# When float64 weights are converted, and in what order the first operations run, in a chain of memory attention and two expert layers

## The chip, the cores and the metric

The kernel runs on one core of a Trainium2 chip. The metric is device time in microseconds (us) from one execution of the whole program. Five engines work beside each other, each with an instruction queue of its own: TensorE (PE: matmuls, and PEld: their weight loads), VectorE (DVE), ScalarE (ACT), GpSimd (POOL) and SyncE (SP), which here only issues transfers (DMAs).

## The reference

Three layers follow each other, on 8 batches of 576 positions (4608 tokens), 8 heads of 64 and 32 memory slots.

```python
# memory attention, per batch and head
a = exp(phi - max(phi, axis=seq)); a = a / (sum(a, axis=seq) + 1e-9)
k_m = a.T @ k; v_m = a.T @ v                    # 32 x 64 each
s = softmax(q @ k_m.T / 8)                      # 576 x 32
x = s @ v_m                                     # heads side by side: 4608 x 512
# first expert layer, d_ff 2048
h = x @ w_in; g = h - tanh(h); x = g @ w_out
# second expert layer, d_ff 768
out = max(max(x @ w1, x @ w2), x @ w3) @ w_out2
```

q, k, v and phi are float32. All weights are float64 in memory, and the program itself must bring them to float32.

## The kernel before, in words

**Precision.** Main matmuls are done with operands split into a high and a low part, three matmuls for one product (`mm3`, lines 94 to 96).

**Weights.** `conv` converts one 128 x 512 block of float64: a load of its raw words (line 115), an absolute value on ScalarE (line 120), five integer and float passes on VectorE (lines 122 to 128) and one sum on GpSimd. For a split weight there follow a copy on ScalarE (line 135) and a subtraction on GpSimd (line 137); for W_in the sum is the result (line 131). It is a generator: each `yield` ends a step. Its tiles `raw`, `cva` and `cvb` have two buffers each.

**Attention.** For each batch `phi_gen` makes exp(phi), `kv_mm` makes K and V of the memory (lines 217 and 221) and their transposes, and `q_gen` makes half a batch of scores (line 106) and their softmax; its result `at` is split and also stored to memory. x is never formed in the first layer: `vw_gen` multiplies V of the memory by W_in (V W_in, line 106) so that h is `at` times `vw` (`ps_h`).

**First expert layer.** d_ff is done in two halves of 8 blocks (`fc`). All tokens pass the first half of W_in and W_out while attention runs, and all pass the second half afterwards, with `at` read back (`at_load`); the partial result goes to memory between (`xd`). A step is one block of one token tile: `emit_h` makes h, `emit_g` the tanh part (lines 433 to 437), `emit_x` the product with W_out (`ps_x`). This is the span up to 897 us; the second half starts near 560 us.

**Second expert layer (the last stage, 897 us to the end).** For each tile of 512 tokens, `emit_max` makes six groups of three products of 12 matmuls each (`ps_w`) and their maximum (lines 624 to 629), and `emit_out` four products with the second W_out (`ps_o`).

**Order.** The program is written once, as a list; an automatic scheduler with a time model of its own orders each engine's instructions from it, earlier ones in the list first where several are ready. What stands where in the list is set by hand: two tracks of generators (`fg` for attention and V W_in, `bg` for conversions) are advanced by `slot()` so many steps (`rate`, in quarters) after every piece of a main step, or run to the end where their result is needed (`need`). A generator may have a gate: the main step before which it does not start.

**Where conversions stand before the change.** The first quarter of W_in is converted in the start (`wi_conv(0)`), W_out's first block after it, and W_out's blocks 1 to 7 and the second quarter of W_in in the first main steps. From the first step of batch 2 on, `last_w` converts all weights of the second expert layer (24 blocks of 384 columns of W1 to W3, 6 of 512 of the second W_out) through one staging tile `cs` with a single buffer, and stores them to memory (line 333, three stores for a block of W1 to W3, and line 339). Behind the attention of the last batch come the third and fourth quarter of W_in and blocks 8 to 15 of W_out (`wo1`), and the rest of `last_w` after them. GpSimd's queue loads the finished weights of the last stage (lines 591, 608 and 612).

```python
    load_phi(0)
    load_kv(0)
    load_q(0, 0)
    load_q(0, 1)
    drain(phi_gen(0))
    drain(chain(kv_mm(0), q_gen(0, (0,))), wi_conv(0))
    drain(vw_gen(0, 0, 0))
```

`drain` advances its generators in turn, a step of each.

Of the kernel before, what the change touches and what calls it, by code (L numbers as in the profile page):

```python
# [22 lines left out]
def kernel(  # L23
# [26 lines left out]
    P = 128  # L50
# [49 lines left out]
    freed = [None, None]  # L100
# [4 lines left out]
    def small(mms):  # L105
        ins = [T.matmul(o, w, x, start=True, stop=True).ins for o, w, x in mms]
        if freed[1] is not None:
            tc.add_manual_dep(ins[0], freed[1].name, mybir.DependencyInfo(mybir.DependencyClass.Sync, mybir.DependencyReason.DATA), reason="both banks")
        for a, b in zip(ins, ins[1:]):
            tc.add_manual_dep(b, a.name, mybir.DependencyInfo(mybir.DependencyClass.NoSync, mybir.DependencyReason.DATA), reason="side by side")  # L110


    def conv(src, n, hi, lo=None):
        raw = cv_p.tile([P, 512, 2], U32, tag="raw", bufs=2, name="raw")
        DMA.dma_start(out=raw[:, :n].rearrange("p c t -> p (c t)"), in_=src.bitcast(U32))
        yield
        a = cv_p.tile([P, 512], U32, tag="cva", bufs=2, name="cva")[:, :n]
        b = cv_p.tile([P, 512], U32, tag="cvb", bufs=2, name="cvb")[:, :n]
        hw, lw = raw[:, :n, 1], raw[:, :n, 0]
# [15 lines left out]
        S.copy(hi, f(a))  # L135
        yield
        G.tensor_sub(lo, f(a), f(hi))  # L137
# [3 lines left out]
    wi = {}  # L141

    def wi_conv(fq):
        t = wo1.tile([P, HP, FQ], F32, name="wi2") if fq == 2 else wi_p.tile([P, HP, FQ], F32, tag="wi", bufs=2, name="wi")
        for r in range(HP):
            yield from conv(moe_w_in[r * P:(r + 1) * P, fq * FQ:(fq + 1) * FQ], FQ, t[:, r])
        wi[fq] = t

# [20 lines left out]
    def load_q(b, g):  # L169
        if b < B and (b, g) not in q_t:  # L170
            t = ap.tile([P, 2, TJ, 32], F32, tag="q", bufs=2, name="qt")
            src = q[b, 4 * g:4 * g + 4].rearrange("(r e) (p j) (t d) -> e t r p j d", e=2, p=32, t=2)
            for e in range(2):
                for h in range(2):
                    for r in range(2):
                        DMA.dma_start(out=t[64 * e + 32 * h:64 * e + 32 * h + 32, r], in_=src[e, h, r])  # L176
            q_t[b, g] = t
# [31 lines left out]
    def kv_mm(b):  # L209
# [15 lines left out]
        load_phi(b + 1)  # L225
        load_kv(b + 1)
# [23 lines left out]
    def q_gen(b, hfs):  # L250
        if 0 in hfs:
            load_q(b, 0)
            load_q(b, 1)
            at_t[0, b] = at_p.tile([P, 2, 2, NS], F32R, tag="at", bufs=3, name="at")
            at_d[b] = dram.tile([P, 2, 2, NS], F32, name=f"at_d{b}")
# [45 lines left out]
    def vw_gen(ph, b, fq):  # L301
        while 2 * ph + fq not in wi:
            bg.need("wi2")
# [15 lines left out]
    def wo_conv(fc, p):  # L319
        t = p.tile([P, 2, DM], F32R, name=f"wo{fc}")  # L320
        yield from conv(moe_w_out[fc * P:(fc + 1) * P, :], DM, t[:, 0], t[:, 1])
# [3 lines left out]
    wb_d = [dram.tile([P, 3, KD, 2, P], F32, name=f"wb_d{j}") for j in range(J)]  # L325
    wz_d = [dram.tile([P, 2, DM], F32, name=f"wz_d{j}") for j in range(J)]

    def wb_conv(w, kc, g):
        t = cv_p.tile([P, 2, 512], F32R, tag="cs", bufs=1, name="cs")
        src = (moe2_w1, moe2_w2, moe2_w3)[w]  # L330
        yield from conv(src[kc * P:(kc + 1) * P, g * 384:(g + 1) * 384], 384, t[:, 0, :384], t[:, 1, :384])
        for i in range(3):
            DMA.dma_start(out=wb_d[3 * g + i][:, w, kc], in_=f(t[:, :, i * P:(i + 1) * P]))
        yield

    def wz_conv(j):
        t = cv_p.tile([P, 2, 512], F32R, tag="cs", bufs=1, name="cs")
        yield from conv(moe2_w_out[j * P:(j + 1) * P, :], DM, t[:, 0], t[:, 1])
        DMA.dma_start(out=wz_d[j], in_=f(t))
        yield  # L340


    class Track:
# [14 lines left out]
        def need(self, name):  # L358
            if any(x[0] == name for x in self.q):
                while self.q:  # L360
# [4 lines left out]
                    if nm == name:  # L365
                        break

# [144 lines left out]
    last_w = [wb_conv(w, kc, g) for g in range(2) for w in range(3) for kc in range(KD)] + [wz_conv(j) for j in range(J)]  # L512
# [30 lines left out]
    for g in last_w:  # L543
        bg.add("last", g, start[0, 2])
# [59 lines left out]
    b_p = pool("b", stack=last2)  # L604
    ps_b = pool("ps_b", PSUM, last2)
    for j in range(2, J):
        wb.append(wb_p.tile([P, 3, KD, 2, P], F32R, name=f"wb{j}"))
        G.dma_start(out=wb[j], in_=wb_d[j])
    wz = []
    for j in range(J):  # L610
        wz.append(wb_p.tile([P, 2, DM], F32R, name=f"wz{j}"))
        G.dma_start(out=wz[j], in_=wz_d[j])
    m_t = {}

    def emit_max(i, j):
        xh = x_t[i]
        pss = []
        for w in range(3):
            ps = ps_b.tile([P, NT], F32, tag=f"w{w}", bufs=2, name=f"ps_w{w}")
# [3 lines left out]
        m = b_p.tile([P, NT], F32, tag="m", bufs=3, name="m")  # L623
# [8 lines left out]
    def emit_out(i, u):  # L632
        ps = ps_b.tile([P, DM], F32, tag="o", bufs=2, name="ps_o")
# [4 lines left out]
        ob = b_p.tile([P, DM], F32, tag="ob", bufs=3, name="ob")  # L638
# [50 lines left out]
```

## Time and profile before

| what | value |
|---|---|
| median of 3 runs | 1499.49 us (1498.4 to 1499.52) |
| profiled execution, its own time | 1499.77 us |
| its span, first to last instruction | 1498.0 us |
| mean granted TensorE clock | 0.975 |
| busy: PE, PEld, DVE, ACT, POOL | 1369.6, 1131.2, 645.1, 419.8, 461.5 us |

All views are of the one profiled execution. Times are counted from the start of its span. An engine is busy while it runs an instruction; what it waited for is inferred from semaphores. The granted clock is a share of full speed: 1.00 is 2.4 GHz, and its lower level is 1.2 GHz. Matmuls overlap in the records, so the end of one is not the start of the next.

### The profile page before, as it was taken

Reading aid. Unit: us, or ns where it says so; the run is one execution under the profiler, and the core shown is the slowest. Engines: PE = TensorE matmul, PEld = TensorE weight load, DVE = VectorE, ACT = ScalarE, POOL = GpSimd, SP = SyncE. Lnnn points to the kernel's source line nnn. Section 1 sums busy time; section 2 is a strip of 40 time slices with the busy share of each in tenths; the row PEclk is TensorE's granted clock in tenths of the full one; section 3 lists DMA queues with packets and bytes.
Section 4 is the critical chain, followed back from the end, with each engine's and each line's share of the span. In section 5 each row is a group of like instructions: output and inputs, shape, how many; then the busy total and the mean of one; then the engine's idle time right before and its main releaser. Section 6 shows DMA issues by size and latency. Waiting matters only on the chain.

```text
span 1498.0 us, 21579 instructions
## 1 busy us (share of the span) xinstructions
PE 1369.6 (91%) x8672; PEld 1131.2 (76%) x8672; DVE 645.1 (43%) x1043; ACT 419.8 (28%) x817; POOL 461.5 (31%) x420
## 2 busy tenths in 40 slices
PE   2575988889998888999999999999999999999998
PEld 1354867677786666788898998888888888888887
DVE  3888787875447994642323222211212121211111
ACT  1323344343343353442323322111111111111110
POOL 0446555543335574543232332111111111111110
PEclk9977899999999998999999999999999999999999
DMA  8565878766432346642312227101101010110001
GB/s 208 142 192 142 230 214 233 210 173 162 120 118 79 129 157 207 209 155 78 113 47 85 75 73 272 36 15 46 46 14 43 15 47 17 43 35 15 15 14 43
DMA packets 190068, 159.75 MB, mean 107 GB/s; under 512 B 95248, under 2 KB 163856, under 8 KB 188176
## 3 DMA queue, kind: packets, MB, share of 16 engines
q1 hardware_dynamic: 188240, 145.79, 33.5%
q0 software_dynamic: 1728, 12.58, 2.3%
q8 instruction: 68, 1.11, 0.3%
q14 instruction: 32, 0.26, 0.1%
HBM read 105.64 MB, written 52.69 MB: 106 GB/s over the span
## 4 chain that ended last, share of the span: by engine, by line
PE 66%; DVE 13%; DMA 8%; SPq 5%; issue 3%; POOL 3%; ACT 2%; DVEq 0%; ACTq 0%; POOLq 0%
PE ps_w L96 10%; PE ps_w L95 10%; PE ps_w L94 10%; PE ps_x L94 5%; PE ps_x L95 5%; PE ps_x L96 5%; DMA wb_d<-cs 3%; PE ps_o L95 3%; PE ps_o L94 3%; PE ps_o L96 3%; PE ps_h L94 3%; PE ps_h L96 3%; PE ps_h L95 3%; DVE cvb L125 2%; SPq L176 2%
## 5 line engine op out<-in xcount | busy, mean ns | idle before, releaser
L437 POOL TENSOR_TENSOR gh<-th,gh 128x320 fp32r<-128x320 f32 (+2 forms) x200 | 209.7, 1050 | 320.3 <-ACT gh L436 311.4
L95 PE MATMUL ps_x<-gh,wo 128*128 128x320 f32 (+2 forms) x800 | 271.0, 341 | 6.7 <-POOL gh L437 6.5
L94 PE MATMUL ps_x<-gh,wo 128*128 128x320 f32 (+2 forms) x800 | 257.0, 343 | 11.8 <-ACT gh L436 6.6
L96 PE MATMUL ps_x<-gh,wo 128*128 128x320 f32 (+2 forms) x800 | 265.6, 335 | 0.7 <-POOL wo L137 0.7
L96 PE MATMUL ps_w<-xh,wb 128*128 128x512 f32 x648 | 255.0, 394 | 0.0
L95 PE MATMUL ps_w<-xh,wb 128*128 128x512 f32 x648 | 254.5, 393 | 0.0
L94 PE MATMUL ps_w<-xh,wb 128*128 128x512 f32 x648 | 253.9, 392 | 0.0
L629 POOL TENSOR_TENSOR mh<-m,mh 128x512 fp32r<-128x512 f32 x54 | 69.8, 1295 | 490.3 <-ACT mh L628 490.3
L434 DVE TENSOR_TENSOR th<-ps_h,th 128x320 f32<-128x320 f32 (+2 forms) x200 | 106.4, 534 | 197.8 <-ACT th L433 197.7
L94 PE MATMUL ps_h<-at,vw 128*128 128x320 f32 (+2 forms) x512 | 160.1, 313 | 32.5 <-DVE th L434 20.9
L94 PEld LDWEIGHTS ps_x<-gh,wo 128*128 128x128 f32 x800 | 150.8, 194 | 38.9 <-issue 17.7
L95 PEld LDWEIGHTS ps_x<-gh,wo 128*128 128x128 f32 x800 | 154.5, 193 | 27.9 <-POOL gh L437 14.5
L96 PEld LDWEIGHTS ps_x<-gh,wo 128*128 128x128 f32 x800 | 153.8, 193 | 10.9 <-issue 1.0
L625 DVE TENSOR_TENSOR m<-ps_w,m 128x512 f32<-128x512 f32 x54 | 37.3, 691 | 283.0 <-PE ps_w L96 283.0
L96 PE MATMUL ps_h<-at,vw 128*128 128x320 f32 (+2 forms) x512 | 155.5, 305 | 1.0 <-DVE vw L312 1.0
L95 PE MATMUL ps_h<-at,vw 128*128 128x320 f32 (+2 forms) x512 | 155.1, 303 | 0.0
L94 PEld LDWEIGHTS ps_h<-at,vw 128*128 128x128 f32 x512 | 100.4, 196 | 62.7 <-DVE th L434 35.6
L436 ACT CAST gh<-th 128x320 fp32r<-128x320 f32 (+2 forms) x200 | 99.7, 499 | 162.4 <-DVE th L434 150.6
L433 ACT ACTIVATE th<-ps_h 128x320 f32<-128x320 f32 (+2 forms) x200 | 94.8, 476 | 177.1 <-PE ps_h L96 168.8
L95 PEld LDWEIGHTS ps_w<-xh,wb 128*128 128x128 f32 x648 | 121.7, 188 | 27.8
L94 PEld LDWEIGHTS ps_w<-xh,wb 128*128 128x128 f32 x648 | 121.8, 188 | 27.5
L96 PEld LDWEIGHTS ps_w<-xh,wb 128*128 128x128 f32 x648 | 121.7, 188 | 27.1
(80 smaller groups left out, 1714.5 us busy)
## 6 DMA issues: line engine op xcount, KB each, us to landing
raw<-in_moe_w_out_dram SPq DMA_DIRECT2D x22, 512.0 KB, 3.5
qt<-in_q_dram SPq DMA_DIRECT2D x128, 72.0 KB, 3.0
at_d<-at SPq DMA_DIRECT2D x16, 576.0 KB, 3.5
raw<-in_moe_w_dram SPq DMA_DIRECT2D x24, 384.0 KB, 3.4
wb_d<-cs SPq DMA_DIRECT2D x72, 128.0 KB, 3.6
at<-at_d SPq DMA_DIRECT2D x8, 1152.0 KB, 5.6
wb<-wb_d POOLq DMA_DIRECT2D x6, 1536.0 KB, 9.3
xr<-xd SPq DMA_DIRECT2D x36, 256.0 KB, 2.9
```

What stands on the lines that cost most here:

```text
L94: T.matmul(o, w[0], x[0], start=start, stop=False)
L95: T.matmul(o, w[0], x[1], start=False, stop=False)
L96: T.matmul(o, w[1], x[0], start=False, stop=stop)
L125: V.scalar_tensor_tensor(out=b, in0=hw, scalar=0xC0000000, in1=b, op0=ALU.bitwise_and, op1=ALU.bitwise_or)
L176: DMA.dma_start(out=t[64 * e + 32 * h:64 * e + 32 * h + 32, r], in_=src[e, h, r])
L433: S.activation(th, ps, AF.Tanh)
L434: V.tensor_sub(th, ps, th)
L436: S.copy(gh[:, 0], th)
L437: G.tensor_sub(gh[:, 1], th, f(gh[:, 0]))
L625: V.tensor_max(m, pss[1], m)
L629: G.tensor_sub(mh[:, 1], m, f(mh[:, 0]))
```

## The change

- **The start.** Everything up to the first V W_in stands in a block whose order is kept as written on every engine. A small Exp on a constant goes first. The first two blocks of W_in are loaded before k and v, q is loaded in two halves, and the last two blocks of W_in are loaded between these halves. The loads of phi, k and v for batch 1 stand after `kv_mm(0)`, as before, but written out. The conversions of W_in are interleaved with `phi_gen`, with nothing, and with `q_gen`.
- **`conv`.** One more `yield` after the load, so every conversion has one more step; a block may now also be gathered as 4 x 128 columns.
- **W_out's second half.** Its 8 blocks are converted where `last_w` stood, go through `cs` to memory, and are loaded from there where they used to be converted.
- **Weights of the last stage.** Blocks are now 128 columns of d_ff by all of d_model (512 wide as before for the second W_out). Groups 0 to 2 of W1 to W3 (9 conversions) are converted in the second half of the first expert layer, staged and loaded as before; groups 3 to 5 (9) and the second W_out (6) are converted in the last stage itself, straight into their tiles, six steps of `bg` before each product.
- **Rates and buffers.** `bg` runs at 6 quarters in place of 8 behind the last attention. In the last stage the conversion tiles are in that stage's own pool, and `m` and `ob` have 2 buffers in place of 3.

```diff
-    freed = [None, None]
+    freed, by_hand = [None, None], [True]
...
         ins = [T.matmul(o, w, x, start=True, stop=True).ins for o, w, x in mms]
+        if by_hand[0]:
+            return
...
-    def conv(src, n, hi, lo=None):
-        raw = cv_p.tile([P, 512, 2], U32, tag="raw", bufs=2, name="raw")
-        DMA.dma_start(out=raw[:, :n].rearrange("p c t -> p (c t)"), in_=src.bitcast(U32))
+    cv = [cv_p]
+
+    def conv(src, hi, lo=None):
+        raw = cv[0].tile([P, 512, 2], U32, tag="raw", bufs=2, name="raw")
+        u = src.bitcast(U32)
+        DMA.dma_start(out=raw.rearrange("p (k c) t -> p k (c t)", k=u.shape[1]) if len(u.shape) == 3 else raw.rearrange("p c t -> p (c t)"), in_=u)
+        yield
         yield
...
-    wi = {}
+    wi, wi_done = {}, set()
-    def wi_conv(fq):
+    def wi_conv(fq, rows=range(HP)):
...
-    def load_q(b, g):
-        if b < B and (b, g) not in q_t:
-            t = ap.tile([P, 2, TJ, 32], F32, tag="q", bufs=2, name="qt")
+    def load_q(b, g, j=slice(TJ)):
+        if b < B:
+            t = q_t[b, g] if (b, g) in q_t else ap.tile([P, 2, TJ, 32], F32, tag="q", bufs=2, name="qt")
...
-        load_phi(b + 1)
-        load_kv(b + 1)
+        if b:
+            load_phi(b + 1)
+            load_kv(b + 1)
...
-    wb_d = [dram.tile([P, 3, KD, 2, P], F32, name=f"wb_d{j}") for j in range(J)]
-    wz_d = [dram.tile([P, 2, DM], F32, name=f"wz_d{j}") for j in range(J)]
-
-    def wb_conv(w, kc, g):
-        t = cv_p.tile([P, 2, 512], F32R, tag="cs", bufs=1, name="cs")
+    wo_d = [dram.tile([P, 2, DM], F32, name=f"wo_d{fc}") for fc in range(FC)]
+
+    def wo_store(fc):
+        t = cv_p.tile([P, 2, DM], F32R, tag="cs", bufs=1, name="cs")
+        yield from conv(moe_w_out[(FC + fc) * P:(FC + fc + 1) * P, :], t[:, 0], t[:, 1])
+        DMA.dma_start(out=wo_d[fc], in_=f(t))
+        yield
+
+    def wo_load(fc):
+        t = wo_t[FC + fc] = wo1.tile([P, 2, DM], F32R, name=f"wo{FC + fc}")
+        DMA.dma_start(out=f(t), in_=wo_d[fc])
+        yield
+
+    JP = 3
+    wb_d = [dram.tile([P, 3, KD, 2, P], F32, name=f"wb_d{j}") for j in range(JP)]
+
+    def wb_conv(w, j, t=None):
+        o = cv_p.tile([P, KD, 2, P], F32R, tag="cs", bufs=1, name="cs") if t is None else t[:, w]
         src = (moe2_w1, moe2_w2, moe2_w3)[w]
-        yield from conv(src[kc * P:(kc + 1) * P, g * 384:(g + 1) * 384], 384, t[:, 0, :384], t[:, 1, :384])
-        for i in range(3):
-            DMA.dma_start(out=wb_d[3 * g + i][:, w, kc], in_=f(t[:, :, i * P:(i + 1) * P]))
-        yield
-
-    def wz_conv(j):
-        t = cv_p.tile([P, 2, 512], F32R, tag="cs", bufs=1, name="cs")
-        yield from conv(moe2_w_out[j * P:(j + 1) * P, :], DM, t[:, 0], t[:, 1])
-        DMA.dma_start(out=wz_d[j], in_=f(t))
-        yield
+        yield from conv(src[:, j * P:(j + 1) * P].rearrange("(k p) c -> p k c", p=P), o[:, :, 0], o[:, :, 1])
+        if t is None:
+            DMA.dma_start(out=wb_d[j][:, w], in_=f(o))
+            yield
+
+    def wz_conv(j, t):
+        yield from conv(moe2_w_out[j * P:(j + 1) * P, :], t[:, 0], t[:, 1])
...
-    load_phi(0)
-    load_kv(0)
-    load_q(0, 0)
-    load_q(0, 1)
-    drain(phi_gen(0))
-    drain(chain(kv_mm(0), q_gen(0, (0,))), wi_conv(0))
-    drain(vw_gen(0, 0, 0))
+    with tc.manual_schedule():
+        S.activation(ones[:, :1], ones[:, :1], AF.Exp, scale=0.0)
+        load_phi(0)
+        c0, c1 = wi_conv(0, range(1)), wi_conv(0, range(1, 2))
+        next(c0)
+        next(c1)
+        load_kv(0)
+        load_q(0, 0, slice(JH))
+        load_q(0, 1, slice(JH))
+        drain(phi_gen(0), c0)
+        drain(c1)
+        c2, c3 = wi_conv(0, range(2, 3)), wi_conv(0, range(3, 4))
+        next(c2)
+        next(c3)
+        load_q(0, 0, slice(JH, TJ))
+        load_q(0, 1, slice(JH, TJ))
+        drain(kv_mm(0))
+        load_phi(1)
+        load_kv(1)
+        drain(q_gen(0, (0,)), chain(c2, c3))
+        drain(vw_gen(0, 0, 0))
+    by_hand[0] = False
...
-    last_w = [wb_conv(w, kc, g) for g in range(2) for w in range(3) for kc in range(KD)] + [wz_conv(j) for j in range(J)]
...
-    for g in last_w:
-        bg.add("last", g, start[0, 2])
+    for fc in range(FC):
+        bg.add("wos", wo_store(fc), start[0, 2])
...
-    bg.q, rest = bg.q[:1], bg.q[1:]
     bg.add("wi2", wi_conv(2))
-    bg.add("wo1", chain(*[wo_conv(fc, wo1) for fc in range(8, 16)]))
-    bg.q += rest
-    rate[1] = 8
+    bg.add("wo1", chain(*[wo_load(fc) for fc in range(FC)]))
+    for j in range(JP):
+        for w in range(3):
+            bg.add("wb", wb_conv(w, j), start[1, 0])
+    rate[1] = 6
...
+    cv[0] = b_p
...
         wb.append(wb_p.tile([P, 3, KD, 2, P], F32R, name=f"wb{j}"))
-        G.dma_start(out=wb[j], in_=wb_d[j])
-    wz = []
+        if j < JP:
+            G.dma_start(out=wb[j], in_=wb_d[j])
+        else:
+            for w in range(3):
+                bg.add(("wb", j), wb_conv(w, j, wb[j]))
     for j in range(J):
         wz.append(wb_p.tile([P, 2, DM], F32R, name=f"wz{j}"))
-        G.dma_start(out=wz[j], in_=wz_d[j])
+        bg.add("wz", wz_conv(j, wz[j]))
     m_t = {}
+    LR = 6
 
     def emit_max(i, j):
         xh = x_t[i]
         pss = []
+        bg.need_all(("wb", j))
         for w in range(3):
+            for _ in range(LR):
+                bg.step(10 ** 9)
...
-        m = b_p.tile([P, NT], F32, tag="m", bufs=3, name="m")
+        m = b_p.tile([P, NT], F32, tag="m", bufs=2, name="m")
...
     def emit_out(i, u):
+        bg.need_all("wz")
...
-        ob = b_p.tile([P, DM], F32, tag="ob", bufs=3, name="ob")
+        ob = b_p.tile([P, DM], F32, tag="ob", bufs=2, name="ob")
```

## Rows read from the trace of the kernel before

**Rows 1.** Table by stretches: us, length, busy PE PEld DVE ACT POOL, PEclk, DMA, GB/s.

```profile
0.00:55.75 55.75, 17.36 (x204) 7.26 (x205) 27.11 (x42) 7.64 (x12) 9.54 (x14) 1.00 0.89 213
55.75:160.00 104.25, 71.58 (x555) 57.47 (x556) 88.17 (x146) 38.66 (x81) 56.06 (x48) 0.79 0.53 149
160.00:335.00 175.00, 153.47 (x1469) 126.94 (x1468) 138.17 (x246) 72.10 (x154) 91.97 (x88) 0.96 0.78 216
335.00:450.00 115.00, 110.62 (x1188) 94.06 (x1187) 59.01 (x102) 43.89 (x89) 39.83 (x38) 1.00 0.48 130
450.00:560.00 110.00, 92.45 (x573) 71.24 (x573) 99.77 (x135) 45.99 (x90) 67.40 (x54) 0.97 0.36 118
560.00:650.00 90.00, 80.91 (x489) 67.50 (x489) 53.42 (x87) 36.46 (x74) 47.64 (x43) 0.94 0.66 221
650.00:897.30 247.30, 247.30 (x1613) 220.05 (x1612) 70.40 (x130) 82.19 (x164) 75.07 (x75) 1.00 0.23 78
897.30:947.00 49.70, 49.70 (x217) 40.38 (x216) 11.22 (x18) 8.91 (x15) 10.66 (x13) 1.00 0.59 217
947.00:1498.00 551.00, 546.18 (x2378) 446.29 (x2376) 97.86 (x143) 83.93 (x143) 63.35 (x49) 1.00 0.11 30
```

**Rows 2.** Timeline of the first 56 us: start, duration, engine, line, operation.

```profile
8.85 15.32 SPq L176 DMA_DIRECT2D qt<-in_q_dram  x16
...
15.87 2.52 PE L221 MATMUL ps_kv<-kv,phi 128*32 128x128 f32 x40 [0.27 <-DMA kv<-in_v_dram]
...
24.21 1.09 SPq L115 DMA_DIRECT2D raw<-in_moe_w_in_dram  x2
...
33.46 2.35 DVE L186 TENSOR_REDUCE mx<-phi 128x256 f32<-128x1280 f32 x1
...
33.73 1.21 PE L106 MATMUL sc<-qT,kT 64*32 64x288 f32 x16 [0.52 <-ACT vT L240]
...
36.79 0.77 DVE L262 STREAM_TRANSPOSE qT<-qt 128x576 f32<-128x576 f32 x1
...
46.90 1.74 POOL L293 TENSOR_TENSOR at<-aT,at 128x576 fp32r<-128x576 f32 x1 [2.48 <-ACT at L292]
...
55.75 0.61 PE L94 MATMUL ps_h<-at,vw 128*128 128x288 f32 x1 [0.67 <-ACT vw L310]
```

**Rows 3.** Groups by line, VectorE, 0 to 56 us: busy us, mean ns, idle before.

```profile
L123 DVE TENSOR_SCALAR cvb<-cva 128x512 uint32<-128x512 uint32 x4 | 3.8, 941 | 0.0
L125 DVE SCALAR_TENSOR_TENSOR cvb<-raw,cvb 128x512 uint32<-128x512 uint32 x4 | 3.7, 923 | 0.1
L128 DVE SCALAR_TENSOR_TENSOR cva<-raw,cva 128x512 f32<-128x512 uint32 x4 | 2.7, 677 | 0.0
L122 DVE TENSOR_SCALAR cva<-cva 128x512 f32<-128x512 f32 x4 | 1.7, 421 | 2.6 <-ACT cva L120 2.6
L127 DVE TENSOR_SCALAR cva<-cvb 128x512 uint32<-128x512 uint32 x4 | 1.7, 414 | 0.1
```

**Rows 4.** The same groups, VectorE, 500 to 560 us.

```profile
L125 DVE SCALAR_TENSOR_TENSOR cvb<-raw,cvb 128x512 uint32<-128x512 uint32 x8 | 9.9, 1234 | 0.2
L123 DVE TENSOR_SCALAR cvb<-cva 128x512 uint32<-128x512 uint32 x8 | 8.8, 1100 | 0.2
L128 DVE SCALAR_TENSOR_TENSOR cva<-raw,cva 128x512 f32<-128x512 uint32 x9 | 8.1, 901 | 0.2
L127 DVE TENSOR_SCALAR cva<-cvb 128x512 uint32<-128x512 uint32 x8 | 6.5, 818 | 0.2
L122 DVE TENSOR_SCALAR cva<-cva 128x512 f32<-128x512 f32 x8 | 6.4, 794 | 0.9 <-ACT cva L120 0.9
```

**Rows 5.** The same view, ScalarE line 135, 160 to 335 us.

```profile
L135 ACT CAST cs<-cva 128x384 fp32r<-128x384 f32 x17 | 8.7, 513 | 36.6 <-DMA wb_d<-cs 36.6
```

**Rows 6.** Waits of TensorE, 560 to 650 us: total us, times, longest.

```profile
PE ps_x L94 <- ACT gh L436: 6.6, 1, 6.6
```

**Rows 7.** Raw tile of the conversions: its loads from issue to landing.

```profile
DMA to landing us min/median/max: 3.0/3.9/13.2
```

More of the change, by code (lines that the diff above doesn't have):

```diff
@@ L110, in small @@
             tc.add_manual_dep(b, a.name, mybir.DependencyInfo(mybir.DependencyClass.NoSync, mybir.DependencyReason.DATA), reason="side by side")
-    def conv(src, n, hi, lo=None):
-        raw = cv_p.tile([P, 512, 2], U32, tag="raw", bufs=2, name="raw")
-        DMA.dma_start(out=raw[:, :n].rearrange("p c t -> p (c t)"), in_=src.bitcast(U32))
+    cv = [cv_p]
[3 more added lines that the diff above has]
+        DMA.dma_start(out=raw.rearrange("p (k c) t -> p k (c t)", k=u.shape[1]) if len(u.shape) == 3 else raw.rearrange("p c t -> p (c t)"), in_=u)
         yield
-        a = cv_p.tile([P, 512], U32, tag="cva", bufs=2, name="cva")[:, :n]
-        b = cv_p.tile([P, 512], U32, tag="cvb", bufs=2, name="cvb")[:, :n]
-        hw, lw = raw[:, :n, 1], raw[:, :n, 0]
+        yield
+        a = cv[0].tile([P, 512], U32, tag="cva", bufs=2, name="cva")
+        b = cv[0].tile([P, 512], U32, tag="cvb", bufs=2, name="cvb")
+        hw, lw = raw[:, :, 1], raw[:, :, 0]
         S.activation(f(a), f(hw), AF.Abs)
@@ L134, in conv @@
         G.tensor_add(f(a), f(b), f(a))
-        S.copy(hi, f(a))
+        x = f(a).rearrange("p (k c) -> p k c", k=hi.shape[1]) if len(hi.shape) == 3 else f(a)
+        S.copy(hi, x)
         yield
-        G.tensor_sub(lo, f(a), f(hi))
+        G.tensor_sub(lo, x, f(hi))
         yield
-    wi = {}
-    def wi_conv(fq):
-        t = wo1.tile([P, HP, FQ], F32, name="wi2") if fq == 2 else wi_p.tile([P, HP, FQ], F32, tag="wi", bufs=2, name="wi")
-        for r in range(HP):
-            yield from conv(moe_w_in[r * P:(r + 1) * P, fq * FQ:(fq + 1) * FQ], FQ, t[:, r])
+    wi, wi_done = {}, set()
+    def wi_conv(fq, rows=range(HP)):
+        t = wi[fq] if fq in wi else wo1.tile([P, HP, FQ], F32, name="wi2") if fq == 2 else wi_p.tile([P, HP, FQ], F32, tag="wi", bufs=2, name="wi")
         wi[fq] = t
+        for r in rows:
+            yield from conv(moe_w_in[r * P:(r + 1) * P, fq * FQ:(fq + 1) * FQ], t[:, r])
+        wi_done.add((fq, rows[-1]))
     phi_t, kv_t, q_t = {}, {}, {}
@@ L175, in load_q @@
                     for r in range(2):
-                        DMA.dma_start(out=t[64 * e + 32 * h:64 * e + 32 * h + 32, r], in_=src[e, h, r])
+                        DMA.dma_start(out=t[64 * e + 32 * h:64 * e + 32 * h + 32, r, j], in_=src[e, h, r][:, j])
             q_t[b, g] = t
@@ L301, in vw_gen @@
     def vw_gen(ph, b, fq):
-        while 2 * ph + fq not in wi:
+        while (2 * ph + fq, HP - 1) not in wi_done:
             bg.need("wi2")
@@ L320, in wo_conv @@
         t = p.tile([P, 2, DM], F32R, name=f"wo{fc}")
[L321 removed]
+        yield from conv(moe_w_out[fc * P:(fc + 1) * P, :], t[:, 0], t[:, 1])
         wo_t[fc] = t
[L325 to L340 removed]
+    wo_d = [dram.tile([P, 2, DM], F32, name=f"wo_d{fc}") for fc in range(FC)]
[12 more added lines that the diff above has]
+        o = cv_p.tile([P, KD, 2, P], F32R, tag="cs", bufs=1, name="cs") if t is None else t[:, w]
+        src = (moe2_w1, moe2_w2, moe2_w3)[w]
+        yield from conv(src[:, j * P:(j + 1) * P].rearrange("(k p) c -> p k c", p=P), o[:, :, 0], o[:, :, 1])
[4 more added lines that the diff above has]
+        yield from conv(moe2_w_out[j * P:(j + 1) * P, :], t[:, 0], t[:, 1])
     class Track:
@@ L366, in need, with need_all @@
                         break
+        def need_all(self, name):
+            while any(x[0] == name for x in self.q):
+                self.need(name)
     fg, bg = Track(), Track()
```

3 lines of the change are left out of this document (1 added, 2 removed).

## The prediction

> **What bounds the kernel now.** I read the table by stretches first, because busy shares over the whole span mix stages with different limits. The stretches are cut at the first main matmul (55.75 us), at places where the background work changes, and at the start of the last stage (897.3 us). The reader is to see in [rows 1] that TensorE is busy for all of 650 to 947 us, at clock 1.00, and for 546 of the 551 us after that. Those 848 us are bound by TensorE, and nothing done on another engine can shorten them. TensorE's idle time is the first column less the second: 38.4 us before the first main matmul, 32.7 us to 160, 21.5 to 335, 4.4 to 450, 17.6 to 560, 9.1 to 650 and 4.8 at the very end, 128 us in all. VectorE is busy for 88 of 104 us, 138 of 175 and 100 of 110 in the stretches where TensorE idles most, and for 59 of 115 where it hardly idles. So in front of 650 us the limit is VectorE together with the waits it passes on.
>
> The granted clock adds to this. Its mean of 0.79, 0.96, 0.97 and 0.94 in four stretches of [rows 1] means that 44, 14, 7 and 11 us ran at the lower level of 1.2 GHz, all of it in the stretches where TensorE pauses. With TensorE busy 70 to 90% there, about 15, 6, 3 and 5 us of work went to the lower clock.
>
> Then I read the order of time in the first stretch [rows 2]. SyncE spends 15.3 us issuing sixteen loads of q before it issues the first loads of W_in at 24.2 us, so VectorE sits idle early (27 us busy of 55.75 [rows 1]) and has conversions and attention work piled up after 30 us. The first scores come at 33.7 us, the attention tile is finished at 46.9 + 1.74 = 48.6 us, and the first main matmul follows at 55.75 us, once V W_in is done.
>
> Last I read what one conversion costs on VectorE: five instructions, 0.42 + 0.94 + 0.92 + 0.41 + 0.68 = 3.38 us in the first stretch [rows 3], and 0.79 + 1.10 + 1.23 + 0.82 + 0.90 = 4.85 us where VectorE and GpSimd are both crowded [rows 4].
>
> **The change, part by part.** The sum is against the profiled execution: 1499.8 us with a span of 1498.0, so 1.8 us lie around the span; the median of the runs is 0.3 us lower.
>
> *The start in fixed order.* Two 512 KB loads of W_in go ahead of k and v, q comes in halves, the Exp table is loaded early, and the other two W_in loads go in front of q's second half. The two early loads, 1.05 MB at the 213 GB/s of the stretch [rows 1], delay k and v by 4.9 us: the first K and V products, which followed the v load at 15.9 us [rows 2], start at 20.8. They take two passes of 2.52 us and a little between, an estimate of 5.6 us. Before, they were so done by 21.5 us, but the scores started only at 33.7, with conversions in front on VectorE. In fixed order the scores follow the few short normalising steps directly, for which I allow 3.5 us: 20.8 + 5.6 + 3.5 = 30 us. From scores to a finished attention tile took 14.9 us before; with two conversions interleaved instead of four and no other batch's reductions, I take 12.5, so 42.5, and V W_in has its weights by then: the first main matmul at about 43.5, a gain of **12 us**. The early end is 18 us (k and v not delayed at all, then 38), the late end 2 us: the third and fourth W_in loads now wait on SyncE's queue for a buffer of the first two, and q's second half, phi and k/v of batch 1 queue behind that wait; if it lasts, V W_in is late instead. The 16 extra issues of q are covered while k and v land.
>
> Work that was done before 55.75 us and is not done before 43.5 now moves behind it: batch 1's maximum, 2.35 us, and two q transposes of 0.77 [rows 2], on a VectorE that is 85% busy there. That gives back **4 us** (0 to 6).
>
> *55.75 to 160 us.* The same twelve W_out and W_in conversions remain; only the following ones change kind. I take **0**, with 10 us either way, since the order of the queues will fall out differently. The extra pause after each conversion's load costs nothing: it only orders the instructions.
>
> *160 to 335 us.* Seventeen 384-wide conversions are here [rows 5]. ScalarE, which also does tanh, waits 36.6 us in all before its copies because the single staging buffer is still being stored. In their place stand eight 512-wide conversions of W_out's second half with one store each: work of eight by 4/3, or 10.7 of 17, and some of it falls before 160 us, so I count 8 of 17. Nine seventeenths of the 21.5 us idle and of the 6 us lost clock are 14.6; I take **-14** (-4 to -22: the staging wait stays for the eight that are left).
>
> *450 to 560 us.* Here W_in's last eight conversions and eight of W_out's second half ran close together. The eight become plain loads of 0.5 MB, 4.2 MB or 20 us of transfer at 213 GB/s, covered by the main matmuls unless W_in's raw loads queue behind them on SyncE. VectorE loses 8 x 4.85 = 39 us of its 100. Of 17.6 us idle plus 3 of clock I take **-12** (-4 to -19), as W_in's conversions still gate V W_in.
>
> *560 to 650 us.* One wait of 6.6 us for ScalarE's copy [rows 6], behind a store of the staging buffer, makes most of the idle time and is followed by the lower clock. The nine conversions left for this half are 512 wide and spaced at a quarter of the former rate; their stores are 9 where there were 72 small ones, and GpSimd's queue issues 3 loads of weights in place of 12. Those loads wait for the stores, and GpSimd's subtraction for the main matmuls queues behind them if a store is late. I take **-9** of 14 (-14 to +5).
>
> *The last stage.* Fifteen conversions, nine for W1 to W3 and six for the second W_out, now run beside matmuls that leave no idle time. The stage has 9 tiles of 6 groups of 36 matmuls plus 36 groups of 18, 2592 in 600.7 us [rows 1], so 8.3 us per group of 36. Group 4 needs 3 conversions by 25 us, group 6 nine by 41.5, and the second product all fifteen by 66 us. VectorE has 11.2 us of its own work per tile [rows 1], 14 us by then. At 3.38 us, 15 conversions and that work end at 65 us: just in time. At 4.85 us they end at 87, 21 us late. The bounds are 0 and 21; I take **+8**, as GpSimd, with two passes per conversion, is about as crowded as in [rows 4], but VectorE can begin in the last steps of the stage before, where it is busy for 70 of 247 us [rows 1], and matmuls of the next tile can be put ahead. The raw loads' median landing is 3.9 us and the worst 13.2 [rows 7]; x of the next tile and the output stores queue behind them on SyncE, with a tile's 50 us and a second buffer in hand. Smaller pools for the maxima and outputs cost nothing at one group per 8.3 us.
>
> By the Trainium skill, "SBUF — State Buffer", section "Who interferes with whom", VectorE and GpSimd share a port pair that whichever starts first holds for its whole instruction. The trace agrees in kind: the mask of line 127 took 0.41 us in [rows 3] and 0.82 in [rows 4]. With every VectorE pass waiting so, the term would be the 64 us of the first rival in place of 8, and the sum +21 in place of -35.
>
> The sum: -12 + 4 - 14 - 12 - 9 + 8 = **-35**; 1498 - 35 + 1.8 gives **1464 us**.
>
> **Rivals.**
> (1) *The last stage waits for its own weights, and the kernel is slower.* Each conversion passes one after the other with VectorE and GpSimd blocking each other. If each of the five passes waits half of a GpSimd pass of 1.74 us [rows 2], a conversion takes 3.38 + 4.35 = 7.7 us, fifteen and the stage's own 14 us end at 130, and TensorE waits 64 us: 1499.8 - 43 + 64 = **1521**. It decides from 6.3 us per conversion, where the wait is 43 us and eats the whole gain. Against it: 4.85 is the worst stretch seen. Chance 0.07.
> (2) *Most of the freed VectorE time is hidden anyway.* The start gains little because k and v come later, and 160 to 650 us keeps its idle time, as attention's own chain (scores, maximum, Exp, sum, transpose) is what TensorE waits for; only half the three middle terms and 5 us at the start remain: 5 + 17 - 8 = 14 us, **1486**. For it: TensorE's waits are many and short. Chance 0.19.
> (3) *The idle time goes altogether between 160 and 650 us*, with its clock (53 + 14), the start gains 18 less 4, and the last stage loses 8: 73 us, **1427**. For it: 335 to 450 us, which has no conversions, idles for only 4.4 of 115. Chance 0.13.
> (4) *The fixed order binds only the start, and the automatic order elsewhere brings the staged conversions back to the same crowded places:* no change, **1499**. Chance 0.04.
>
> **How the numbers follow.** The forecast has 0.57, with a range of its own from 1440 to 1482. About 0.2%, 3 us, is what a measurement of this kernel can tell from none. Faster: 0.57 + 0.19 + 0.13 = 0.89. Same: 0.04. Slower: 0.07. The range goes down to 1434, where half of rival 3 is left out, and up to 1492, which takes in rival 2 and leaves out 4 and 1.
>
> **What would show it.** The first main matmul near 43.5 us, scores near 30. VectorE below 110 us of busy time in what was 160 to 335, ScalarE's staging wait halved. No 6.6 us wait after W_in's last conversion, and a clock of 1.00 from there on. TensorE fully busy from some 90 us after the start of the second half of W_in. In the last stage, a TensorE idle time of some 8 us in the first 66 us, and a stage of about 609 us. The forecast is wrong if the start gains nothing, if the middle keeps its idle time, or if the last stage is more than 21 us longer.

## The result, and the profile of the kernel after

The changed kernel takes 1481.10 us (median of 4 runs, 1479.61 to 1482.18) beside 1499.51 us for the kernel before (4 runs, same chip): a ratio of 0.9878, 95% interval 0.9861 to 0.9895. The gain is 18.4 us where 35 were forecast. The span is 1479.8 us.

To see where it arose, both traces are cut at the same points of the work: the first main matmul, the end of the 3rd, 8th, 11th and 15th token tile of the first half, the start of the second half, and the start of the last stage. A tile ends with its four results `xo`; the first four tiles pass twice, with four blocks each time, and each pass is counted. The kernel before is cut once more at 650 us. Kernel before, from its first main matmul on (columns as in [rows 1]):

```profile
55.75:151.40 95.65, 62.98 (x508) 48.92 (x509) 81.23 (x134) 35.74 (x75) 50.01 (x42) 0.79 0.52 146
151.40:239.90 88.50, 77.98 (x820) 66.89 (x820) 68.61 (x132) 35.02 (x79) 45.01 (x47) 0.89 0.84 237
239.90:339.60 99.70, 88.69 (x728) 73.20 (x728) 79.37 (x130) 43.46 (x89) 54.20 (x50) 1.00 0.68 185
339.60:470.60 131.00, 125.67 (x1327) 106.53 (x1333) 70.71 (x124) 48.63 (x99) 47.65 (x45) 1.00 0.43 119
470.60:560.50 89.90, 73.30 (x410) 54.49 (x394) 85.70 (x112) 38.29 (x75) 58.89 (x46) 0.96 0.43 140
560.50:650.00 89.50, 80.41 (x486) 67.18 (x486) 52.92 (x85) 35.96 (x73) 47.14 (x43) 0.94 0.66 220
```

Kernel after:

```profile
0.00:54.00 54.00, 16.77 (x205) 7.26 (x205) 27.98 (x43) 8.20 (x14) 9.07 (x14) 1.00 0.80 195
54.00:151.90 97.90, 66.29 (x514) 52.78 (x515) 83.41 (x134) 35.22 (x73) 50.45 (x42) 0.72 0.55 158
151.90:240.70 88.80, 70.76 (x783) 61.35 (x783) 69.64 (x119) 33.56 (x73) 44.93 (x42) 0.92 0.82 245
240.70:330.20 89.50, 89.50 (x760) 77.31 (x758) 49.59 (x89) 37.20 (x73) 35.15 (x34) 0.98 0.46 122
330.20:462.10 131.90, 127.18 (x1328) 108.45 (x1334) 70.80 (x124) 48.90 (x100) 47.84 (x45) 0.99 0.43 118
462.10:539.10 77.00, 67.57 (x396) 54.43 (x380) 63.92 (x91) 32.42 (x65) 47.08 (x38) 0.93 0.65 230
539.10:866.90 327.80, 327.80 (x2117) 288.26 (x2112) 103.30 (x186) 114.46 (x227) 106.94 (x104) 1.00 0.31 104
866.90:1479.80 612.90, 600.22 (x2593) 488.75 (x2592) 170.05 (x236) 109.88 (x187) 113.04 (x84) 0.99 0.15 43
```

The second column is the length of a stretch. Their differences, after less before: -1.8, +2.3, +0.3, -10.2, +0.9, -12.9, then 327.8 against 89.5 + 247.3, -9.0, and for the last stage +12.2 (before 1498.0 - 897.3 = 600.7). Together -18.2. So the first 240 us gained nothing, 31 us were won between 240 us and the last stage, and the last stage took 12 back.

The reader should see two things in the stretch from the 8th to the 11th tile (239.90:339.60 before, 240.70:330.20 after). VectorE's busy time fell from 79 to 50 us and TensorE is busy for all of the stretch: the 30 us that left VectorE bought the 11 us that TensorE had idled. In the second half (539.10:866.90) TensorE no longer pauses, and the wait of [rows 6] is gone. ScalarE's wait for the staging store [rows 5] shrank from 36.6 to 2.7 us, between 160 and 330 us:

```profile
L142 ACT CAST cs<-cva 128x512 fp32r<-128x512 f32 x6 | 3.7, 622 | 2.7 <-DMA wo_d<-cs 2.7
```

The timeline of the start, answering to [rows 2]:

```profile
16.34 2.52 PE L229 MATMUL ps_kv<-kv,phi 128*32 128x128 f32 x40 [1.03 <-DMA kv<-in_v_dram]
...
24.73 1.22 PE L106 MATMUL sc<-qT,kT 64*32 64x288 f32 x16 [0.52 <-ACT vT L249]
...
30.62 0.81 DVE L282 STREAM_TRANSPOSE s<-sc 128x288 f32<-128x288 f32 x2
...
33.83 0.78 DVE L269 STREAM_TRANSPOSE qT<-qt 128x576 f32<-128x576 f32 x1 [2.09 <-DMA qt<-in_q_dram]
...
36.98 2.31 DVE L194 TENSOR_REDUCE mx<-phi 128x256 f32<-128x1280 f32 x1 [2.37 <-DMA phi<-in_phi_dram]
...
39.81 0.75 DVE L285 TENSOR_REDUCE st<-s 128x18 f32<-128x576 f32 x1
...
47.01 1.50 POOL L300 TENSOR_TENSOR at<-aT,at 128x576 fp32r<-128x576 f32 x1 [1.75 <-ACT at L299]
...
50.46 1.92 PE L106 MATMUL ps_w<-wi,vT 64*32 64x512 f32 x4 [7.18 <-POOL wi L137]
...
53.99 0.61 PE L94 MATMUL ps_h<-at,vw 128*128 128x288 f32 x1 [1.62 <-ACT vw L317]
```

The scores come at 24.7 us, nine earlier than before and five earlier than forecast. Their transposes (`s`, line 282) are done at 31.4. Then line 285, the next step of the softmax, should follow; it runs at 39.8. In between VectorE stood 2.09 us for the second half of q, and 2.37 us for phi of batch 1. Both of these instructions belong to work that the program writes **behind** the block with the fixed order. The block keeps the order of its own instructions; it does not keep the automatic scheduler from placing later ones in the gaps its time model sees, and where the data then come late, everything queued behind on VectorE waits. The conversions of W_in stand in the same queue: V W_in waits for the fourth block to 50.46 us, and the first main matmul follows V W_in, not the attention tile, which is finished at 48.5.

### The profile page after: what moved, and what is told of

The parts are those of the page before. It is cut to its first block, busy times and chain, and to the rows that moved or that the text cites. A ratio compares the mean times of both kernels' runs of the same rounds, so it can differ in the third digit from the quotient of the medians.

```text
span 1479.8 us, 21379 instructions
## 1 busy us (share of the span) xinstructions
PE 1366.1 (92%) x8672; PEld 1138.6 (77%) x8672; DVE 638.7 (43%) x1013; ACT 419.8 (28%) x806; POOL 454.5 (31%) x399
## 4 chain that ended last, share of the span: by engine, by line
PE 75%; DVE 11%; DMA 4%; SPq 4%; issue 3%; POOL 2%; ACT 1%; DVEq 0%; POOLq 0%; ACTq 0%
PE ps_w L96 9%; PE ps_w L95 8%; PE ps_w L94 8%; PE ps_x L94 8%; PE ps_x L95 8%; PE ps_x L96 8%; PE ps_h L94 4%; PE ps_h L96 4%; PE ps_h L95 4%; PE ps_o L95 3%; PE ps_o L96 3%; PE ps_o L94 3%; SPq L184 3%; PE ps_w L106 2%; DVE cvb L131 2%
## 5 line engine op out<-in xcount | busy, mean ns | idle before, releaser
L459 POOL TENSOR_TENSOR gh<-th,gh 128x320 fp32r<-128x320 f32 (+2 forms) x200 | 204.3, 1023 | 366.2 <-ACT gh L458 347.7
L94 PEld LDWEIGHTS ps_w<-xh,wb 128*128 128x128 f32 x648 | 122.4, 189 | 31.8 <-ACT wb L142 4.4
```

Of the source, the lines that this page charges most:

```text
L94: T.matmul(o, w[0], x[0], start=start, stop=False)
L459: G.tensor_sub(gh[:, 1], th, f(gh[:, 0]))
```

## The experiments

All are variants of one of the two kernels; their ratios are against the kernel before on the same chip. Its medians on these chips are 1499.5 to 1503.4 us, so differences between medians of different chips are good to some 4 us. The expectations count **marks**: mark 1 is the first main matmul, and each end of the four `xo` copies of a token tile is one more, so their fourth and ninth tile are the ends of the 3rd and the 8th token tile.

| kernel | median us | ratio, 95% interval | first main matmul | start of last stage |
|---|---|---|---|---|
| before with the new start | 1495.11 | 0.9965 (0.9952 to 0.9979) | 55.1 | 892.4 |
| after with the old start | 1466.52 | 0.9782 (0.9756 to 0.9807) | 56.0 | 853.1 |
| after, later work held back | 1474.42 | 0.9834 (0.9807 to 0.9862) | 43.9 | 854.1 |
| after, all last weights staged | 1484.32 | 0.9896 (0.9873 to 0.9919) | 55.6 | 881.2 |
| the same at a lower rate | 1485.10 | 0.9886 (0.9853 to 0.9919) | 55.3 | 883.5 |
| all staged, paced | 1460.34 | 0.9725 (0.9704 to 0.9747) | 55.3 | 857.4 |
| old start, all staged, paced | 1448.73 | 0.9647 (0.9624 to 0.9670) | 55.1 | 845.1 |
| after, start ordered automatically | 1457.53 | 0.9702 (0.9677 to 0.9727) | 50.5 | 843.5 |
| before, new start ordered automatically | 1479.55 | 0.9850 (0.9827 to 0.9873) | 50.1 | 875.4 |
| held back, W_out staged later | 1467.73 | 0.9769 (0.9746 to 0.9792) | 44.2 | 850.7 |
| automatic start, all staged, paced | 1438.51 | 0.9577 (0.9554 to 0.9600) | 49.8 | 835.9 |
| the same, W_out staged later | 1441.01 | 0.9593 (0.9570 to 0.9617) | 48.8 | 837.1 |

**The two halves of the change apart.** First the new start alone, in the kernel before:

```diff
-    load_phi(0)
...
-    drain(vw_gen(0, 0, 0))
+    with tc.manual_schedule():
...
+        drain(vw_gen(0, 0, 0))
```

> The kernel before with the new start alone (fixed order, W_in ahead of k and v, q in halves); all weights stay where they were. Theory A (the fixed block gains nothing, because three VectorE instructions of later work are put into its gaps and wait there for transfers): first main matmul at 53 to 55 us, total within 4 us of the kernel before, 1496 to 1503. Theory B (the start does bring its time, and the moved conversions lose it again before 240 us): total 8 to 14 us shorter, 1485 to 1492.

Then the moved weights alone, by the opposite edit of the kernel after:

> The changed kernel with the start of before; all moved conversions stay. Theory A: 1478 to 1485 us, no different from the changed kernel beyond 4 us. Theory B: 1489 to 1495 us.

Measured: 1495.1 and 1466.5. The start alone is worth 5 us, between the two theories; the weights alone 33; together they give 18. The second kernel fits no theory on record: putting the **old** start back made the changed kernel 15 us faster. The parts do not add; the fixed start costs the moved weights 15 us. The trace of the kernel with the old start says where. Its second, third and fourth stretch by the same cuts:

```profile
56.00:146.70 90.70, 63.15 (x520) 49.69 (x521) 80.19 (x131) 35.23 (x73) 46.97 (x41) 0.74 0.53 152
146.70:231.10 84.40, 71.34 (x808) 59.29 (x807) 70.17 (x122) 32.84 (x74) 42.86 (x42) 1.00 0.87 251
231.10:321.30 90.20, 87.13 (x729) 74.89 (x727) 51.79 (x89) 37.49 (x73) 37.49 (x34) 0.98 0.49 133
```

Beside the kernel before these are -5.0, -4.1 and -9.5 us; with the fixed start they were +2.3, +0.3 and -10.2.

**Is it the later work in the block's gaps?** What is written behind the block, up to the eighth main step, is queued on VectorE behind the block's last VectorE instruction and on ScalarE behind its last ScalarE instruction; this sets order only.

```diff
     by_hand[0] = False
+    held = ExitStack()
+    held.enter_context(tc.issue_after(freed[1]))
+    held.enter_context(tc.issue_after(act_last[0]))
     drain(wo_conv(0, wo_p), q_gen(0, (1,)))
...
-    run(0, start[0, 2])
+    run(0, 8)
+    held.close()
+    run(8, start[0, 2])
```

> The changed kernel, but what follows the fixed block is queued behind its last instruction on VectorE and on ScalarE (order only, no wait). Theory A: the scores' maximum starts some 8 us earlier, the first main matmul at 45 to 47 us, and the total is 3 to 9 us shorter than the changed kernel (1472 to 1478). Rival C (VectorE has the same work up to 240 us, so an earlier start is waited away): first main matmul earlier as well, but the tile that ended at 241 us ends within 2 us of that, total 1479 to 1483.

Its timeline of the start:

```profile
28.89 0.84 DVE L282 STREAM_TRANSPOSE s<-sc 128x288 f32<-128x288 f32 x2
...
30.69 0.74 DVE L285 TENSOR_REDUCE st<-s 128x18 f32<-128x576 f32 x1
...
37.89 1.52 POOL L300 TENSOR_TENSOR at<-aT,at 128x576 fp32r<-128x576 f32 x1 [1.75 <-ACT at L299]
```

Line 285 now follows line 282 by 1.8 us in place of 9.2, and the first main matmul comes at 43.9 us. That shows what made the start late. The median fell by 7 us (1474.4), as theory A said. The traced execution is the fastest of the four (1468.8 us), and it keeps the 10 us: its 8th token tile ends at 231.1 us in place of 240.7, and its last stage starts at 854.1 in place of 866.9, so rival C is out. But 231.1 us is also where that tile ends with the old start, whose first main matmul comes 12 us later. An early first matmul is worth little by itself: what follows waits for something else.

**What it waits for.** TensorE's longest wait between the 2nd and the 3rd token tile of the kernel before, of after, and of the one held back:

```profile
PE ps_h L94 <- ACT at L292: 10.8, 1, 10.8
```
```profile
PE ps_h L94 <- ACT at L299: 10.9, 1, 10.9
```
```profile
PE ps_h L94 <- ACT at L299: 10.5, 1, 10.5
```

It is the attention tile of batch 1, and it is late in all three; with the old start in the kernel after the same wait is 10.0 us. So the start was left as the change writes it, but taken out of the fixed order, in the kernel after and in the kernel before:

```diff
-    with tc.manual_schedule():
+    with ExitStack():
```

> The changed kernel with the same start text, but not fixed: the automatic scheduler orders it. So far the old start with the moved weights ran 15 us faster than the changed kernel. Theory E (the fixing itself costs: on VectorE later work is put into the block's gaps in the order of the scheduler's time model, in which k, v and q land sooner than on the chip): total 1464 to 1474. Theory F (the loads cost: W_in ahead of k and v, and 32 half loads of q in front of batch 1 and of W_out's first blocks): total 1478 to 1485, as fixed.

> The kernel before with the new list of the start, but ordered automatically (the weights stay where they were). Theory E, fixing the order is itself what costs: the gain of 24 us that freeing the start gave the changed kernel does not need the moved weights, so this kernel ends 13 to 27 us under the one with the fixed start alone (1495), at 1468 to 1482, and the fourth tile of the first half ends by 137 us against 154.8. Rival K, the cost comes only from how the start's order meets the moved conversions: within 6 us of the fixed start alone, 1489 to 1500, the fourth tile after 148 us.

Measured: 1457.5 and 1479.6. In both kernels the same list, ordered automatically, is faster: by 23.6 us of median with the moved weights, more than theory E had, and by 15.6 without, as it had (ratios 0.9702 beside 0.9878, and 0.9850 beside 0.9965). Fixing the order is what costs, wherever the weights are. The stretch from the 2nd to the 3rd token tile in the kernel before with the fixed and with the automatic start:

```profile
114.20:154.80 40.60, 23.18 (x129) 18.11 (x130) 35.02 (x58) 15.43 (x33) 25.72 (x22) 0.66 0.51 137
```
```profile
103.90:129.70 25.80, 18.03 (x117) 15.47 (x117) 25.05 (x37) 12.68 (x28) 15.46 (x13) 0.90 0.42 144
```

Fifteen us less, with a granted clock of 0.90 in place of 0.66, and there is no 10 us wait in it; the longest for `ps_h` is

```profile
PE ps_h L94 <- DVE th L438: 3.0, 1, 3.0
```

The chain of batch 1 is earlier by more than the start is. Its transposed K (`kT`) is copied at 96.25 us with the fixed start and at 73.82 with the automatic one (both in the kernel before):

```profile
96.25 0.25 ACT L246 COPY kT<-ps_t 128x128 f32<-128x128 f32 x1
```
```profile
73.82 0.27 ACT L246 COPY kT<-ps_t 128x128 f32<-128x128 f32 x1 [1.60 <-PE ps_t L243]
```

An early `kT` is not enough, though. With the later work held back it came early too, but the scores of batch 1 followed it by 16.7 us, and the 10.5 us wait stayed:

```profile
77.14 0.26 ACT L249 COPY kT<-ps_t 128x128 f32<-128x128 f32 x1
...
93.83 0.72 PE L106 MATMUL sc<-qT,kT 64*32 64x288 f32 x16
```

In the changed kernel ordered automatically the two stand at 75.00 and 84.84 us, 9.8 us apart. In the start the order differs as well: the automatic one converts W_in's blocks before the softmax, and V W_in runs at 41.84 us in place of 50.46.

So the new list of the start, ordered automatically, is worth 22 us in the kernel before (1501.5 to 1479.6 on one chip), of which the fixed block leaves 5. With the moved weights it is worth some 9 by the medians (1466.5 to 1457.5) and 12 by the ratios, and the fixed block turns that into a loss of 15. Which of the differences in order brings how much was not isolated.

**The last stage.** Do the 15 conversions there cost what they save? All 24 are staged in the second half instead:

```diff
-    JP = 3
+    JP = 6
...
+    for j in range(J):
+        bg.add("wb", wz_conv(j), start[1, 0])
...
-    rate[1] = 2
+    rate[1] = 3
...
-        bg.add("wz", wz_conv(j, wz[j]))
+        G.dma_start(out=wz[j], in_=wz_d[j])
```

> The changed kernel with all fifteen conversions taken out of the last stage: groups 3 to 5 and the second W_out are converted and staged in the second half of the first expert layer too, 24 conversions there in place of 9. Theory A (the 12 us that the last stage grew are waits on its own conversions and the lower clock after them): last stage 600 to 603 us, second half unchanged, total 1467 to 1472. Rival D (the single staging buffer makes ScalarE wait in the second half, and the 12 us only move there): second half 8 us longer or more, total 1477 to 1484.

The last stage takes 600.9 us, as before the change: the 12 us are those conversions. But the second half grew by as much, 341.5 us beside 327.8; the total is rival D's, and whether its reason holds the next run tells. Two edits were then tried against that, a paced one (every background step in the second half is queued behind the newest tanh subtraction, and the rate is 2), and the lower rate alone:

```diff
+                with tc.issue_after(th_last[0]) if paced[0] and i else ExitStack():
                     tr.step(now[0])
...
-        V.tensor_sub(th, ps, th)
+        th_last[0] = V.tensor_sub(th, ps, th).ins
```

> As the run with all conversions staged (which ran 1484 us with a last stage of 601 and a second half 14 us longer), but each background step's VectorE work is queued behind the newest tanh subtraction of the main steps, and its rate is 2 quarters in place of 3, so that the 24 conversions spread over the second half. Theory G (the second half lost its 14 us because the scheduler ran the conversions as fast as their buffers allowed, and they pushed the tanh work back): second half 326 to 331 us, last stage 600 to 603, total 1466 to 1472. Rival D (ScalarE waits for the one staging buffer whatever the pace): second half 335 us or more, total above 1476.

> All conversions staged in the second half as in the first staged kernel, at rate 2 in place of 3, and not queued behind the tanh subtraction: it tells apart the two edits of the paced kernel (1460.3, second half 326.6 us). Theory G1, the queueing does it, since the automatic order draws conversions forward wherever the list has them: second half 336 to 345 us, 1476 to 1486. Rival G2, the lower rate does it: second half 325 to 331 us, 1458 to 1466.

Measured: 1460.3 and 1485.1. The lower rate alone does nothing; the queueing, at that rate, does all of it, and rival D's single buffer was not the reason. The first 100 us of the second half and the whole of it, staged without pace:

```profile
539.70:640.00 100.30, 93.02 (x564) 76.96 (x563) 74.62 (x114) 44.57 (x90) 60.24 (x50) 0.98 0.71 241
539.70:881.20 341.50, 332.71 (x2107) 288.58 (x2106) 163.92 (x261) 128.82 (x257) 151.90 (x135) 1.00 0.42 143
```

and paced:

```profile
531.80:632.00 100.20, 100.20 (x672) 87.02 (x671) 56.36 (x97) 43.92 (x88) 49.54 (x46) 1.00 0.60 203
531.80:857.40 325.60, 325.60 (x2130) 288.19 (x2129) 171.83 (x292) 136.17 (x266) 164.01 (x147) 1.00 0.49 167
```

Without pace VectorE has 75 us of work in the first 100 and TensorE gets 564 matmuls through; paced it has 56, and TensorE gets 672. Over the whole half VectorE does rather more (172 us against 164). The place in the list did not set the pace: the automatic order drew the conversions forward until TensorE had to pause.

The paced kernel is 6 us under the range of theory G, and the marks say why. Of the 21 us that it gains over the changed kernel, 12 are in the last stage, 2 in the second half, and 9 between the 15th tile and the second half, 68.0 us beside 77.0 (it was 2 us behind up to there):

```profile
463.80:531.80 68.00, 63.19 (x379) 51.98 (x364) 38.89 (x59) 27.94 (x54) 30.24 (x26) 0.95 0.49 177
```

For the changed kernel had the same fault. Eight of its nine loads of W1 to W3, written for the second half, are issued in front of it, and six of the nine conversions pass VectorE there, beside six of W_in; paced, only W_in's six are left:

```profile
L120 SPq DMA_DIRECT2D raw<-in_moe_w_dram x8: 367/373/384, 492.4 to 534.8; - x8
```

**Both together.** The pace with the old start, and with the new start ordered automatically:

> The old start with the moved weights (1466.5 us) and the 24 paced staged conversions. Theory G: 12 us less in the last stage and no more in the second half, 1452 to 1458. Rival D: 1462 or more.

> The changed kernel with its start ordered automatically, and all last-stage conversions staged in the second half, paced behind the tanh subtraction. Theory G, the pace and the start are separate terms: 1457.5 less the 18 to 21 us that pacing gave with the other two starts, 1435 to 1441, last stage 601 us. Rival: the start's gain of 10 us over the old start is waited away when the second half is the bound, 1446 to 1451 as with the old start.

Measured: 1448.7 and 1438.5. Against the same kernels without staging and pace that is 17.8 and 19.0 us (the first 3 us under theory G's range); the pace is a term of its own. The second, 0.9577 of the kernel before (0.9554 to 0.9600), is the fastest kernel of this study and faster than the change as made by 43 us.

**What did not help.** Conversions of W_out's second half crowd VectorE in front of 231 us, so they were gated to the fourth batch, and paced, first with the later work held back, then on the fastest kernel:

```diff
-        bg.add("wos", wo_store(fc), start[0, 2])
-    rate[:] = 6, 2
+        bg.add("wos", wo_store(fc), start[0, 4])
+    rate[:] = 6, 3
+    paced[0] = True
```

> The held start, with the eight conversions of W_out's second half begun at batch 4 in place of batch 2 and paced as above, so that VectorE has none of them before some 235 us. Theory H (an earlier start is waited away up to 231 us because VectorE is crowded there by conversions): the tile that ended at 231 us in the held start ends 6 to 14 us earlier, and the total is 1458 to 1468. Rival I (attention's own chain sets the pace up to there): that tile ends at 228 to 232, total 1470 to 1477.

> The same, with the staging of W_out's second half gated to the fourth batch and paced too. Theory H, conversions in front of 220 us are what VectorE lacks time for: the ninth tile ends near 205 us in place of about 221, and half of that is given back after 360 us as it was before, so 1425 to 1434. Rival: all of it is given back, or more, because 8 staged conversions now stand close to the eight of W_in: 1436 to 1448.

On the fastest kernel the stretch up to the 8th token tile fell from 91.6 to 72.8 us, and all of it came back by 510 us (the 15th tile ends at 510.3 and 511.5 us). Without and with the later gate:

```profile
129.70:221.30 91.60, 76.10 (x817) 64.31 (x816) 79.49 (x132) 36.53 (x78) 49.96 (x46) 0.93 0.81 240
```
```profile
129.70:202.50 72.80, 66.37 (x754) 59.38 (x753) 41.96 (x82) 26.40 (x58) 28.01 (x31) 0.93 0.61 165
```

VectorE's busy time from 129.7 to 510 us is 242.7 and 242.9 us: the same work later is the same work. So here the rival held. With the later work held back the 8th tile ended 19 us earlier (211.7 in place of 231.1) and 7 us were left of it at the end (1474.4 to 1467.7, on two chips), as theory H had it.

## Why the prediction was right, and where it was wrong

The direction and the range held, and 1481 lies at the edge of the forecast's own 1440 to 1482. Step by step:

- **The start, forecast -12, measured -1.8.** This is the step that failed, in the sentence "with two conversions interleaved instead of four and no other batch's reductions, I take 12.5". It was 23.8 us from the scores at 24.7 to a finished tile at 48.5, since another batch's reduction and another half's transposes do stand in there, and wait for their loads. The half sentence "and V W_in has its weights by then" failed too, as V W_in stood last. Where the later work was held back the first main matmul came at 43.9, beside 43.5 forecast, but by luck: the scores came at 25.0 in place of 30, the tile took 14.4 us in place of 12.5, and V W_in then kept the matmul waiting from 39.4 us on, where 1 us was allowed. The other price in that step, 4.9 us of delay for k and v, did not appear either: the products start at 16.3, after 15.9 before.
- **The work carried back, +4, and 55.75 to 160 us, 0.** Measured together +2.3 up to the 3rd token tile. The prediction took the stretch's 33 us of idle time to stay and did not ask what it is: a third of it is one wait of 10.8 us for batch 1's attention. With the automatic start it is gone.
- **160 to 335 us, -14, measured +0.3 - 10.2 = -9.9.** Within its bounds. With the old start the same two stretches give -4.1 - 9.5 = -13.6, so the size was right for the moved weights, and the 4 us missing belong to the fixed start.
- **450 to 560 us, -12, measured -12.9.** Right in size, in part by luck. VectorE lost 21.8 us (85.7 to 63.9) where 39 were forecast: W_out's eight conversions left, but six of W1 to W3, which the prediction had in the second half at a quarter of the former rate, came in their place. Where the pace kept these out the stretch took 68.0 us, 21.9 less than before and beyond the bound of -19.
- **560 to 650 us, -9, measured -9.0.** Right: the wait of [rows 6] went.
- **The last stage, +8, measured +12.2.** The idle time rose by 12.7 - 4.8 = 7.9 us, as forecast; the term left out the clock. TensorE's waits at the stage's start (866.9 to 947 us):

```profile
PE ps_w L94 <- ACT wb L142: 3.5, 2, 2.8
PE ps_o L94 <- ACT wz L142: 3.2, 1, 3.2
```

and the granted clock from 900 us on, after 1.00 in the 15 us before:

```profile
900.00:915.00 15.00, 11.52 (x44) 8.43 (x43) 12.75 (x17) 4.93 (x9) 9.69 (x8) 0.93 0.33 105
915.00:933.00 18.00, 18.00 (x75) 14.46 (x75) 17.55 (x20) 6.49 (x11) 10.62 (x9) 0.96 0.33 114
933.00:960.00 27.00, 22.82 (x91) 17.90 (x90) 23.06 (x29) 9.57 (x17) 18.20 (x13) 0.94 0.24 80
```

In these stretches part of the time runs at the lower level (1.2 GHz), and the busy time of the stage is 600.2 us, 4.3 more than the 49.70 + 546.18 = 595.9 us of [rows 1].

The rivals: the first, that the last stage waits for its own weights, needed 6.3 us per conversion on VectorE. In the first twelve, up to 935 us, it was 0.94 + 0.92 + 0.83 + 0.77 + 0.69 = 4.15, between [rows 3] and [rows 4]:

```profile
L131 DVE SCALAR_TENSOR_TENSOR cvb<-raw,cvb 128x512 uint32<-128x512 uint32 x12 | 11.3, 943 | 0.3
L133 DVE TENSOR_SCALAR cva<-cvb 128x512 uint32<-128x512 uint32 x12 | 11.0, 916 | 0.2
L129 DVE TENSOR_SCALAR cvb<-cva 128x512 uint32<-128x512 uint32 x12 | 9.9, 829 | 0.2
L134 DVE SCALAR_TENSOR_TENSOR cva<-raw,cva 128x512 f32<-128x512 uint32 x12 | 9.3, 774 | 0.2
L128 DVE TENSOR_SCALAR cva<-cva 128x512 f32<-128x512 f32 x12 | 8.3, 688 | 8.4 <-ACT cva L126 5.6 <-POOL mh L675 2.8
```

The second (1486) is nearest in time, for a reason it did not have: the middle terms came nearly whole (-31.8 of -35), and the start gained little though k and v were not late. The third (1427) would have needed all idle time to go; the fastest variant here goes a good part of that way, to 1438.5. The fourth, that the automatic order brings staged work back to crowded places, was wrong in its time, as 18 us were won, but its mechanism took place: six conversions of W1 to W3 went back in front of the second half, for 9 us, and the staged kernel without pace shows it in full.

By the Trainium skill, "SBUF — State Buffer", section "Who interferes with whom", where VectorE and GpSimd contend, the one that is issued first holds the shared port pair for its whole instruction. The trace of the last stage agrees in kind: over its 15 conversions the mask of line 133 took 0.43 us at the median and 1.51 at most, beside GpSimd's sums of 1.28 to 1.75 us. That every pass pays, as the first rival had it, the trace does not show: 4.15 us stand against 3.38 where it was least crowded.

## What to carry to other kernels

A part of a program with a fixed order still has gaps, and an automatic scheduler may fill them with later work whose data come late: look in the timeline, on the engine that sets the pace, for instructions of other batches, and test by holding those back or by giving the same list back to the scheduler, before the gain of a fixed order is counted. Background work moved to an idle stretch can need an edge in the order that ties it to the main loop: here a place in the list and a rate did not pace it (1485 against 1460 us). And an early first matmul is not yet a gain: what counts is the next wait behind it, here one of 10 to 11 us that stood in each of the kernels read with the old or the fixed start.

## What the runs showed of the hardware that was not expected

Two 512 KB loads put ahead of k and v hardly delayed them: the products waiting for v began 0.5 us later, where their size at the stretch's 213 GB/s gave 4.9, though the mean rate of that stretch was lower, 195 GB/s. And pauses of TensorE in a stage that is otherwise busy cost more than their length: 7.9 us of them in the last stage came with 4.3 us more busy time for the same 2592 matmuls, at granted clocks of 0.93 to 0.96 around them. With the old start it was 9.2 us of pauses and 3.0 us more busy time, so how much more is not fixed.
